# Sigmoid attention interleaved with a seven-product FFN: operands' parts and sums in other slots, PSUM banks kept across the first stage change, another opening

## The chip, the cores and the metric

The kernel runs on one core of one Trainium2 chip. The metric is the device time of one execution in microseconds, as the median of several runs. On a core, TensorE (PE) multiplies matrices, VectorE (DVE) and ScalarE (ACT) work elementwise, GpSimd (POOL) does next to nothing here, and SyncE (SP) issues nearly all DMA transfers. Each engine executes its own instructions in order and waits on semaphores for the others.

## The reference

Shapes: q, k, v are 8 x 12 x 448 x 64 (batch, heads, sequence, head size), w_in is 768 x 2048, w_out 2048 x 768.

```
scores = (1 / sqrt(64)) * q @ k.T - log(448)
attn   = 1 / (1 + exp(-scores))
x      = (attn @ v), heads joined: 3584 x 768
h      = x @ w_in
g      = max(0.01 * h, h)
out    = g @ w_out
```

The weights come in as 64-bit floats; the kernel decodes them on the chip.

## The kernel before, in words

**Precision.** Every operand of a product is split into a high part (a copy rounded to fp32r, ScalarE's `high`) and a low part (the rest, a subtraction, VectorE's `low`), and each product is made as three: high with high, high with low, low with high (`parts_mm`, line 157). For q and k the tile of both parts is `qks`, for the FFN's left operands `so`, for its weights `w`.

**Attention.** Two heads make a pair of 128 partitions; there are 48 pairs, 12 to a quarter. `load_qk` and `load_v` load a pair's operands; `split` (pair 0 alone) or `high` and `low` make the parts of q and k; `scores(h)` makes two tiles of scores (`sc`) and two sigmoids on ScalarE (`s`), `attn_v(h)` the products with v into a bank `pv`, and `keep` copies a finished bank to `x`.

**FFN.** Both products use a scheme over 2 x 2 blocks with seven block products instead of eight, taken in the order 0, 1, 4, 5, 3, 6, 2. The left operand of the first product consists of seven combinations of blocks of x (class `Operands`): operand n has a high part, a low part, and some need a sum first (`sum1`, `sum2`, `sum4`, `s3`). `Quad` gathers the results in the PSUM banks px and pz and adds them up into c11, c21, c22 and c12 (in the trace all named `c_h`): after product 5 ScalarE copies pz into c22, after product 3 VectorE adds px to it, which frees px for product 2. `First.after` then issues the activation, the sums s3, s4, s2 of the results (in the trace `s<-c_h`, `s<-s`) and their stores `g<-c_h`, `g<-s`. A block of nine matmuls is one of the seven products for one of eight column groups u.

**The order.** Attention of quarter q runs between the steps of the first product of quarter q - 1: 56 steps p0 to p55, with slots e0.0 to e12.3 for the pairs; in quarter 0 there is attention alone, and the second product comes after everything. `slot` runs the chores that `later` has put down for it, then its work. The tables `PLAN` (line 473) and `PLAN_ALONE` (line 477, quarter 0) say in which slot a step of `Operands` is issued: `"p50": "h102"` is the high part of operand 1, thirds 0 to 2, in step 50; l is a low part, s a sum, and a key that begins with n is a slot of the next quarter. All instructions are pinned to the order in which the program issues them.

**Weights.** The generator `prep` (line 247) decodes 16 blocks, w_in's and w_out's, on VectorE: each step is one instruction. The raw halves or quarters `wr` become `wd`, then four differences `ws` are made; three parts of `wd` and all of `ws` are stored to DRAM (`t`), from where `Weights` reads them (`wx`). After each block come some empty steps, `WAIT[0]` for the first four blocks, `WAIT[1]` for the others, as the next block takes memory that the stores must have read. The first four blocks' raw parts lie in the buffers of `so`. `prepare` advances the generator by `PACES` steps per slot: the first value in quarter 0, the second until w_in is done, the third behind it.

**Banks and loads.** PSUM has eight banks. In quarter 0 the pool `ps_a` has three tiles of two banks for scores and two for pv; at quarter 1 it is closed and `ps_b` opened, with two score tiles, two pv, px and pz (line 607). At the start (line 566) SyncE issues k of pair 0 in halves, q and k of pair 1, then v_0, v_1, q and k of pair 2 and v_2; ScalarE issues q of pair 0.

Every instruction in the trace has line 90, that of the helper that pins it, so rows are told apart by their tiles.

Of the kernel before, what the change touches and what calls it, by code (L numbers as in the profile page):

```python
# [9 lines left out]
F32 = mybir.dt.float32  # L10
# [6 lines left out]
P = 128  # L17
# [7 lines left out]
ST = 9  # L25
# [1 line left out]
ALONE = 4  # L27


PACES = 1.45, 2.2, 1.33  # L30
WAIT = 2, 4


JOINT_ALONE = 1, 3, 5, 7
# [22 lines left out]
def attn_ffn_kernel(ctx: ExitStack, tc: tile.TileContext, qk, v, w_in, w_out, out):  # L57
# [153 lines left out]

    ps = ExitStack()

    def banks(name, sizes):

        pool = ps.enter_context(tc.tile_pool(name=name, bufs=1, space=PSUM, reuse_waits="tile"))
# [101 lines left out]

    xs = {}

    KEYS = slice(0, S // 2), slice(S // 2, S)
    OTHERWISE = 9

    class Pair:
# [32 lines left out]
        def split(self):  # L357

            self.parts = spl.tile([P, 2, 2, S], F32R, tag="qks", name=f"qks_{self.i}")
            high, low = self.parts[:, 0], self.parts[:, 1]  # L360
            copy(out=high[:, 0], in_=self.raw[:, 0])
            vcopy(out=high[:, 1, KEYS[0]], in_=self.raw[:, 1, KEYS[0]])
            sub(low[:, 0], self.raw[:, 0], high[:, 0])
            for n, cols in enumerate(KEYS):
                if n > 0:
                    vcopy(out=high[:, 1, cols], in_=self.raw[:, 1, cols])
                sub(low[:, 1, cols], self.raw[:, 1, cols], high[:, 1, cols])

        def scores(self, h):
            todo, acts = [], []  # L370
            for c in range(2 * h, 2 * h + 2):
                ps = psum("s", f"sc_{self.i}_{c}")

                if self.part == 0:
                    k0, n, rows = c * KR, KR, slice(0, KR)
                elif c < NK - 1:
                    k0, n, rows = c * P, P, slice(0, P)
                elif self.part == 1:
                    k0, n, rows = S - D, D, slice(0, D)
                else:  # L380
                    k0, n, rows = S - P, P, slice(D, P)
                for m, (kp, qp) in enumerate(((0, 0), (0, 1), (1, 0))):
                    for j, me in enumerate(heads):
                        todo.append((c, m, dict(out=ps[:n, j, :S], lhsT=self.parts[me, kp, 1, k0:k0 + n],
                                                rhs=self.parts[me, qp, 0], start=m == 0, stop=m == 2)))
# [12 lines left out]

        def attn_v(self, h):
            if h == 0:  # L400
                self.pv = psum("pv", f"pv_{self.i}")
# [23 lines left out]
    class Operands:  # L425
# [45 lines left out]


    PLAN = {
# [3 lines left out]
    PLAN_ALONE = {  # L477
# [3 lines left out]


    w1 = []
# [26 lines left out]
    class First:  # L510
# [22 lines left out]
        def after(self, quad, c, u, n):  # L533
            got = quad.done(n)
            if got is None:
                return
            p = self.p
            row, col, t = got
            c[row, col] = t

            def save(n, t):
                dma(out=gd[p][n][:, u], in_=t)

            def sums(n, fn, x, y):
                c[n] = st.tile([P, S], F32, tag="st", name=f"s{n}_{p}_{u}", bufs=ST)
                fn(c[n], c[x], c[y])

            if n != 2:
                later(1, lambda: leaky(t, t))
            if n == 1:  # L550
                later(3, lambda: save(0, t))
            elif n == 3:
                later(3, lambda: save(6, t))
            elif n == 6:
                later(2, lambda: sums(3, add, (1, 0), (1, 1)))
                later(3, lambda: sums(4, sub, 3, (0, 0)))
                later(4, lambda: save(3, c[3]))
                later(4, lambda: sub(t, c[0, 0], t))
                later(5, lambda: save(4, c[4]))
                later(6, lambda: save(5, t))  # L560
            else:
                later(2, lambda: save(1, t))
                later(4, lambda: sums(2, sub, (0, 1), 4))
                later(6, lambda: save(2, c[2]))
# [38 lines left out]
    for q in range(NQ + 1):  # L603
        before, ops = ops, Operands(q) if q < NQ else None
        if q == 0:
            slot(lambda: pairs[0].scores(0))
        elif q == 1:
            ps.close()
            psum = banks("ps_b", dict(s=(2, 2), pv=(2, 1), px=(1, 1), pz=(1, 1)))
        if q == 0:  # L610
            for j in range(per):
                i, busy = j, j == 0 or j >= per - 2
# [24 lines left out]
        for k in range(size):  # L637
# [10 lines left out]
                    later(1, pairs[i + 1].load_v)  # L648
            go(q, f"p{k}", first.step, k >= 50 or k < 7)
    ps.close()  # L650


    KS = 2
# [149 lines left out]
```

## Time and profile before

| | |
|---|---|
| median of 3 runs | 1111.12 us (1110.78 to 1113.02) |
| the profiled execution | 1110.32 us, its span 1108.5 us |
| granted TensorE clock, mean | 0.998 |
| busy: TensorE, VectorE, ScalarE | 1093.0, 666.4, 614.3 us |
| DMA | 250.09 MB, mean 226 GB/s |

The profile is of one execution. A timeline row has start and length in us, the engine, the operation with the tile that it writes and those that it reads, its shape and count, and in brackets the idle time before it with what ended that. Rows of like instructions in a row are drawn together. A row of waits has the waiting engine and tile, what was waited for, the total in us, the count and the longest.

### The profile page before, as it was taken

How to read it: one execution, taken by the hardware profiler on the slowest of the kernel's cores; microseconds unless marked ns; L12 is line 12 of the kernel's file. 1: busy time of each engine (PE TensorE's matmuls, PEld its weight loads, DVE VectorE, ACT ScalarE, POOL GpSimd, SP SyncE). 2: the span in 40 equal slices, each digit the busy share in tenths (PEclk: the TensorE clock that was granted, in tenths of full speed). 3: DMA queues.
4: the chain of work that ended last, by engine and by line, in shares of the span. 5: the costliest groups of instructions: out<-in, count | busy, mean ns of one | idle time of the engine just before them, and what ended most of it. 6: DMA issues, size and time to landing. Idle time of an engine off the chain costs nothing.

```text
span 1108.5 us, 15979 instructions
## 1 busy us (share of the span) xinstructions
PE 1093.0 (99%) x5952; PEld 893.6 (81%) x5952; DVE 666.4 (60%) x987; ACT 614.3 (55%) x862; POOL 0.3 (0%) x5
## 2 busy tenths in 40 slices
PE   8999999999999999999999999999999999999998
PEld 4556767777777777777778899999999999999998
DVE  5889888768676678676568666655433333343332
ACT  7886666677666667665667555554333333323331
POOL 0000000000000000000000000000000000000000
PEclk9999999999999999999999999999999999999999
DMA  7966988885787786777755889786645554454552
GB/s 276 342 205 226 326 282 300 282 280 166 232 287 279 249 253 203 251 262 257 259 200 147 284 265 297 273 287 213 203 142 157 158 171 154 133 176 150 157 149 92
DMA packets 105133, 250.09 MB, mean 226 GB/s; under 512 B 11680, under 2 KB 54816, under 8 KB 105056
## 3 DMA queue, kind: packets, MB, share of 16 engines
q1 hardware_dynamic: 104912, 248.85, 68.2%
q8 instruction: 46, 0.75, 0.3%
q14 instruction: 31, 0.25, 0.1%
q10 hardware_dynamic: 144, 0.23, 0.1%
HBM read 164.63 MB, written 84.41 MB: 225 GB/s over the span
## 4 chain that ended last, share of the span: by engine, by line
PE 92%; DVE 3%; ACT 2%; DMA 1%; issue 1%; SPq 0%; DVEq 0%; ACTq 0%
PE px_o L90 21%; PE px_h L90 19%; PE pv L90 12%; PE sc L90 11%; PE pz_o L90 10%; PE pz_h L90 9%; PE py_o L90 5%; PE py_h L90 5%; ACT s L90 1%; DVE so L90 1%; ACT so L90 1%; DMA t<-wd 1%; DVE w L90 1%; DVE x L90 0%; DMA g<-s 0%
## 5 line engine op out<-in xcount | busy, mean ns | idle before, releaser
L90 DVE TENSOR_TENSOR gs<-gg,gs 128x896 fp32r<-128x896 f32 x112 | 122.2, 1092 | 226.9 <-ACT gs L90 226.7
L90 PE MATMUL px_h<-so,w 128*128 128x448 f32 x1152 | 250.9, 366 | 1.4 <-DVE c_h L90 1.1
L90 PEld LDWEIGHTS px_h<-so,w 128*128 128x128 f32 x1152 | 213.4, 188 | 27.9 <-issue 8.2
L90 PE MATMUL px_o<-gs,w 128*128 128x448 f32 x1152 | 232.5, 362 | 0.0
L90 ACT CAST gs<-gg 128x896 fp32r<-128x896 f32 x112 | 105.3, 941 | 222.5 <-PE px_o L90 117.6
L90 PEld LDWEIGHTS px_o<-gs,w 128*128 128x128 f32 x1152 | 216.0, 187 | 14.4
L90 ACT ACTIVATE s<-sc 128x896 f32<-128x896 f32 (+1 forms) x192 | 171.6, 918 | 72.3 <-PE sc L90 49.4
L90 PE MATMUL sc<-qks 64*128 64x448 f32 (+2 forms) x1152 | 144.0, 385 | 8.0 <-ACT qks L90 4.3
L90 PEld LDWEIGHTS sc<-qks 64*128 64x128 f32 (+2 forms) x1152 | 98.1, 180 | 65.1 <-issue 28.2
L90 DVE TENSOR_TENSOR w<-wx,w 128x768 fp32r<-128x768 f32 (+1 forms) x160 | 136.1, 853 | 16.3 <-ACT w L90 14.7
L90 PE MATMUL pv<-s,v 128*64 128x448 f32 (+2 forms) x768 | 141.9, 551 | 0.0
L90 PE MATMUL pz_h<-so,w 128*128 128x448 f32 x576 | 126.6, 363 | 2.6 <-DVE c_h L90 1.3
L90 ACT CAST w<-wx 128x768 fp32r<-128x768 f32 (+1 forms) x160 | 119.8, 752 | 5.7 <-DMA wx<-t 5.3
L90 PEld LDWEIGHTS pz_h<-so,w 128*128 128x128 f32 x576 | 107.4, 187 | 12.2 <-ACT c_h L90 1.9
L90 PE MATMUL pz_o<-gs,w 128*128 128x448 f32 x576 | 116.5, 362 | 0.0
L90 PEld LDWEIGHTS pz_o<-gs,w 128*128 128x128 f32 x576 | 108.0, 187 | 7.2
L90 PEld LDWEIGHTS pv<-s,v 128*64 128x64 f32 (+2 forms) x768 | 42.8, 135 | 76.7 <-issue 74.6
L90 DVE TENSOR_TENSOR qks<-qk,qks 128x896 fp32r<-128x896 f32 (+2 forms) x50 | 52.5, 1052 | 38.4 <-ACT qks L90 38.3
L90 DVE SCALAR_TENSOR_TENSOR wd<-wr,wd 128x384 int32<-128x384 int32 (+1 forms) x112 | 68.6, 613 | 2.3
L90 ACT COPY c_h<-px_h 128x448 f32<-128x448 f32 x64 | 34.1, 533 | 60.7 <-PE px_h L90 59.8
L90 ACT ACTIVATE c_h<-c_h 128x448 f32<-128x448 f32 x96 | 55.2, 575 | 22.1 <-DVE c_h L90 22.1
L90 PE MATMUL py_h<-so,w 128*128 128x448 f32 x288 | 62.9, 362 | 0.0
(38 smaller groups left out, 663.0 us busy)
## 6 DMA issues: line engine op xcount, KB each, us to landing
gg<-g SPq DMA_DIRECT2D x112, 448.0 KB, 3.5
wx<-t SPq DMA_DIRECT2D x120, 384.0 KB, 4.1
g<-c_h SPq DMA_DIRECT2D x128, 224.0 KB, 4.9
g<-s SPq DMA_DIRECT2D x96, 224.0 KB, 4.9
qk<-in_qk SPq DMA_DIRECT2D x47, 448.0 KB, 5.1
t<-ws SPq DMA_DIRECT2D x16, 768.0 KB, 5.4
wr<-in_w_out SPq DMA_DIRECT2D x32, 384.0 KB, 4.6
out<-c_o SPq DMA_DIRECT2D x48, 224.0 KB, 2.0
```

Source lines behind the costliest of these rows:

```text
L90: return lambda *args, **kw: tc.keep_in_program_order(issue(*args, **kw))
```

## The change

- **Parts and sums.** In `PLAN`, operand 2's high part moves from np3 to np4 and is made in two pieces, its low part from np4 to np4 and np5 in two pieces; a third of the sum for operand 4 that operand 2 rests on moves from np2 to e12.2; sums 1 and 2 are split likewise. In `PLAN_ALONE`, operand 2's high part moves from ne1.0 to ne1.3, its low part from ne1.2 to np4.
- **Results' sums.** For a quarter's last column group, s4, the subtraction into c21, s2 and their stores come four slots later (`LATER`).
- **Weights.** The paces in quarters 1 and later are 2.45 and 1.46 (2.2 and 1.33); seven empty steps follow a block from the fifth on (four).
- **Banks.** pv and two of the score tiles lie in pools of their own, kept from quarter 0 to the end of the first product's attention; only the third score tile's two banks are given to px and pz.
- **Opening.** q and k of pair 0 are loaded in halves, q's by ScalarE, k's by SyncE; pair 1's likewise, q by ScalarE; v_1 and v_2 come behind q and k of pairs 2 and 3. `split` works in halves of columns. Pair 0's first scores are made in halves of columns, the first tile finished ahead of the second. Before them stand seven products of zeros (64 x 112, into a pv bank that is not read).

```
-PACES = 1.45, 2.2, 1.33
-WAIT = 2, 4
+PACES = 1.45, 2.45, 1.46
+LATER = 4
+IDLE = 7
+WAIT = 2, 7
...
             if self.i == 0:
-                dma_act(out=self.raw[:, 0], in_=qk[self.i, :, 0])
-                for cols in KEYS:
-                    dma(out=self.raw[:, 1, cols], in_=qk[self.i, :, 1, cols])
+                for cols in HALVES:
+                    dma_act(out=self.raw[:, 0, cols], in_=qk[self.i, :, 0, cols])
+                    dma(out=self.raw[:, 1, cols], in_=qk[self.i, :, 1, cols])
+            elif self.i == 1:
+                dma_act(out=self.raw[:, 0], in_=qk[self.i, :, 0])
+                dma(out=self.raw[:, 1], in_=qk[self.i, :, 1])
...
-                ps = psum("s", f"sc_{self.i}_{c}")
+                ps = psum_s(self.i * NK + c, f"sc_{self.i}_{c}")
...
+                for cols in HALVES if self.i == h == 0 else (slice(0, S),):
+                    for m, (kp, qp) in enumerate(((0, 0), (0, 1), (1, 0))):
+                        for j, me in enumerate(heads):
+                            todo.append((c, (m > 0 and c + 1, m, cols.start), dict(
...
-        "np0": "h302", "np1": "l302", "np2": "h602 s402", "np3": "l602 h202", "np4": "l202"}
+        "np0": "h302", "np1": "l302", "np2": "h602 s412", "np3": "l602", "np4": "h200 h212 l200", "np5": "l212"}
...
+                z = LATER if u == NU - 1 else 0
-                later(3, lambda: sums(4, sub, 3, (0, 0)))
+                later(3 + z, lambda: sums(4, sub, 3, (0, 0)))
...
+    zeros = st.tile([P, S], F32, tag="st", name="zeros", bufs=ST)[:, :S // 4]
+    nc.vector.memset(zeros, 0.0)
     pairs[0].load_qk()
     pairs[1].load_qk()
     pairs[0].load_v()
-    pairs[1].load_v()
     act(out=warm, in_=warm, func=AF.Sigmoid)
     pairs[0].split()
     pairs[2].load_qk()
+    pairs[1].load_v()
...
-    psum = banks("ps_a", dict(s=(3, 2), pv=(2, 1)))
+    psv = ExitStack()
+    psum_v = banks("ps_v", dict(pv=(2, 1)), psv)
+    psum_two = banks("ps_s", dict(s0=(1, 2), s1=(1, 2)), psv)
+    psum = banks("ps_a", dict(s2=(1, 2)))
+
+    def psum_s(n, name):
+
+        if n < per * NK:
+            return (psum if n % 3 == 2 else psum_two)(f"s{n % 3}", name)
+        return psum_two(f"s{n % 2}", name)
...
         if q == 0:
+            unread = psum_v("pv", "unread")
+            for _ in range(IDLE):
+                mm(unread[heads[0], :S // 4], lhsT=zeros[:, :D], rhs=zeros, start=True, stop=True)
             slot(lambda: pairs[0].scores(0))
         elif q == 1:
             ps.close()
-            psum = banks("ps_b", dict(s=(2, 2), pv=(2, 1), px=(1, 1), pz=(1, 1)))
+            psum = banks("ps_b", dict(px=(1, 1), pz=(1, 1)))
```

ScalarE at the first steps of the first product (quarter 1): c22 is the result block copied from pz, so2_0 operand 2 of quarter 0, s_13_0 to s_13_2 the sigmoids of pair 13. Before:

```order
L90 CAST w0_0_3_1004<-wx0_0_3_801 128x384
L90 COPY c22_h0_0_1016<-pz_h0_0_1006 128x448
L90 CAST so2_0_1020<-x_1_484 128x1344
L90 ACTIVATE s_13_0_1030<-sc_13_0_1022 128x896
L90 ACTIVATE s_13_1_1038<-sc_13_1_1023 128x896
L90 ACTIVATE s_13_2_1069<-sc_13_2_1061 128x896
```

Now:

```order
L92 CAST w0_0_3_1036<-wx0_0_3_833 128x384
L92 COPY c22_h0_0_1048<-pz_h0_0_1038 128x448
L92 ACTIVATE s_13_0_1060<-sc_13_0_1052 128x896
L92 ACTIVATE s_13_1_1068<-sc_13_1_1053 128x896
L92 CAST so2_0_1093<-x_1_516 128x1344
L92 ACTIVATE s_13_2_1103<-sc_13_2_1095 128x896
```

The cast of operand 2 has moved behind two sigmoids.

VectorE at the same place, from the sum for operand 2 (x_1) to the addition into c22; wr0_3, wd0_3 and ws0_3 belong to the fourth weight block. Before:

```order
L90 TENSOR_TENSOR x_1_484<-x_1_484,s2_0_831 128x1344
L90 SCALAR_TENSOR_TENSOR wd0_3_782<-wr0_3_0_595,wd0_3_782 128x768
L90 TENSOR_SCALAR wd0_3_782<-wr0_3_1_664 128x768
L90 TENSOR_SCALAR wd0_3_782<-wd0_3_782 128x768 x2
L90 TENSOR_TENSOR so2_0_1020<-x_1_484,so2_0_1020 128x1344
L90 SCALAR_TENSOR_TENSOR wd0_3_782<-wr0_3_1_664,wd0_3_782 128x768 x2
L90 TENSOR_TENSOR ws0_3_1079<-wd0_3_782 128x384
L90 TENSOR_TENSOR ws0_3_1079<-wd0_3_782,ws0_3_1079 128x384
L90 TENSOR_TENSOR w0_0_3_1004<-wx0_0_3_801,w0_0_3_1004 128x384
L90 TENSOR_TENSOR c22_h0_0_1016<-c22_h0_0_1016,px_h0_0_952 128x448
```

Now:

```order
L92 TENSOR_TENSOR x_1_516<-x_1_516,s2_0_863 128x1344
L92 SCALAR_TENSOR_TENSOR wd0_3_814<-wr0_3_0_627,wd0_3_814 128x768
L92 TENSOR_SCALAR wd0_3_814<-wr0_3_1_696 128x768
L92 TENSOR_SCALAR wd0_3_814<-wd0_3_814 128x768 x2
L92 SCALAR_TENSOR_TENSOR wd0_3_814<-wr0_3_1_696,wd0_3_814 128x768 x2
L92 TENSOR_TENSOR ws0_3_1091<-wd0_3_814 128x384
L92 TENSOR_TENSOR ws0_3_1091<-wd0_3_814,ws0_3_1091 128x384
L92 TENSOR_TENSOR ws0_3_1091<-wd0_3_814 128x384
L92 TENSOR_TENSOR so2_0_1093<-x_1_516,so2_0_1093 128x1344
L92 TENSOR_TENSOR w0_0_3_1036<-wx0_0_3_833,w0_0_3_1036 128x384
L92 TENSOR_TENSOR c22_h0_0_1048<-c22_h0_0_1048,px_h0_0_984 128x448
```

Operand 2's low part has moved behind the weight block's steps, one more ws among them, and the addition stays behind them all.

VectorE at the end of the sixth weight block (wr0_5, wd0_5), whose store is issued behind the last row that writes wd0_5. Before:

```order
L90 TENSOR_TENSOR c21_h0_2_1444<-c21_h0_2_1444,pz_h0_2_1451 128x448
L90 TENSOR_TENSOR qks_18_1547<-qk_18_1312,qks_18_1547 128x896
L90 TENSOR_SCALAR wd0_5_1425<-wd0_5_1425 128x384
L90 SCALAR_TENSOR_TENSOR wd0_5_1425<-wr0_5_3_1462,wd0_5_1425 128x384
L90 TENSOR_TENSOR w0_3_1_1570<-wx0_3_1_1431,w0_3_1_1570 128x2x384
L90 SCALAR_TENSOR_TENSOR wd0_5_1425<-wr0_5_3_1462,wd0_5_1425 128x384
```

Now:

```order
L92 TENSOR_SCALAR wd0_5_1441<-wd0_5_1441 128x384 x2
L92 TENSOR_TENSOR c22_h0_2_1499<-c22_h0_2_1499,px_h0_2_1431 128x448
L92 TENSOR_TENSOR w0_3_0_1567<-wx0_3_0_1429,w0_3_0_1567 128x2x384
L92 SCALAR_TENSOR_TENSOR wd0_5_1441<-wr0_5_3_1477,wd0_5_1441 128x384 x2
L92 TENSOR_TENSOR c21_h0_2_1480<-c21_h0_2_1480,pz_h0_2_1487 128x448
L92 TENSOR_TENSOR qks_18_1584<-qk_18_1347,qks_18_1584 128x896
```

The block's last steps have moved ahead of the addition into c21, a q/k low part and a weight low part.

VectorE where the first product of quarter 3 starts, from the addition into c11 of its column group 0 to that into c22; s4_2_7, s2_2_7 and c21_h2_7 are results of the quarter before. Before:

```order
L90 TENSOR_TENSOR c11_h3_0_6073<-c11_h3_0_6073,py_h3_0_6081 128x448
L90 TENSOR_TENSOR s4_2_7_6092<-s3_2_7_6076,c11_h2_7_5933 128x448
L90 TENSOR_TENSOR x_13_4921<-x_13_4921,s2_3_5987 128x1344
L90 TENSOR_TENSOR w0_0_2_6079<-wx0_0_2_6012,w0_0_2_6079 128x2x384
L90 TENSOR_TENSOR c21_h2_7_5966<-c11_h2_7_5933,c21_h2_7_5966 128x448
L90 TENSOR_TENSOR so6_3_6095<-x_15_5766,so6_3_6095 128x1344
L90 TENSOR_TENSOR s2_2_7_6133<-c12_h2_7_6055,s4_2_7_6092 128x448
L90 TENSOR_TENSOR so2_3_6116<-x_13_4921,so2_3_6116 128x1344
L90 TENSOR_TENSOR w0_0_3_6118<-wx0_0_3_6026,w0_0_3_6118 128x384
L90 TENSOR_TENSOR c22_h3_0_6130<-c22_h3_0_6130,px_h3_0_6063 128x448
```

Now, on to the sum s4 of the quarter before:

```order
L92 TENSOR_TENSOR c11_h3_0_6117<-c11_h3_0_6117,py_h3_0_6125 128x448
L92 TENSOR_TENSOR x_13_4964<-x_13_4964,s2_3_5924 128x896
L92 TENSOR_TENSOR w0_0_2_6123<-wx0_0_2_6054,w0_0_2_6123 128x2x384
L92 TENSOR_TENSOR so6_3_6137<-x_15_5811,so6_3_6137 128x1344
L92 TENSOR_TENSOR so2_3_6171<-x_13_4964,so2_3_6171 128x448
L92 TENSOR_TENSOR w0_0_3_6157<-wx0_0_3_6068,w0_0_3_6157 128x384
L92 TENSOR_TENSOR c22_h3_0_6169<-c22_h3_0_6169,px_h3_0_6107 128x448
L92 TENSOR_TENSOR so2_3_6171<-x_13_4964,so2_3_6171 128x896
L92 TENSOR_TENSOR w0_1_0_6175<-wx0_1_0_6105,w0_1_0_6175 128x2x384
L92 TENSOR_TENSOR c21_h3_0_6152<-c21_h3_0_6152,pz_h3_0_6159 128x448
L92 TENSOR_TENSOR s4_2_7_6205<-s3_2_7_6120,c11_h2_7_5976 128x448
```

Ahead of the addition into c22 the three sums of the quarter before, a third of x_13's sum and two thirds of operand 2's low part are gone.

More of the change, by code (lines that the diff above doesn't have):

```diff
@@ L212, in attn_ffn_kernel, with banks @@
     ps = ExitStack()
-    def banks(name, sizes):
-        pool = ps.enter_context(tc.tile_pool(name=name, bufs=1, space=PSUM, reuse_waits="tile"))
+    def banks(name, sizes, stack=ps):
+        pool = stack.enter_context(tc.tile_pool(name=name, bufs=1, space=PSUM, reuse_waits="tile"))
         def psum(tag, name):
@@ L360, in split @@
             high, low = self.parts[:, 0], self.parts[:, 1]
[L361 to L366, printed above, removed]
+            for cols in HALVES:
+                copy(out=high[:, 0, cols], in_=self.raw[:, 0, cols])
+            for n, cols in enumerate(HALVES):
+                vcopy(out=high[:, 1, cols], in_=self.raw[:, 1, cols])
                 sub(low[:, 1, cols], self.raw[:, 1, cols], high[:, 1, cols])
+                if n == 0:
+                    for x in HALVES:
+                        sub(low[:, 0, x], self.raw[:, 0, x], high[:, 0, x])
         def scores(self, h):
@@ L381, in scores @@
                     k0, n, rows = S - P, P, slice(D, P)
[L382 to L385, printed above, removed]
+                for cols in HALVES if self.i == h == 0 else (slice(0, S),):
+                    for m, (kp, qp) in enumerate(((0, 0), (0, 1), (1, 0))):
+                        for j, me in enumerate(heads):
+                            todo.append((c, (m > 0 and c + 1, m, cols.start), dict(
+                                out=ps[:n, j, cols], lhsT=self.parts[me, kp, 1, k0:k0 + n],
+                                rhs=self.parts[me, qp, 0, cols], start=m == 0 and cols.start == 0,
+                                stop=m == 2 and cols.stop == S, skip_group_check=True)))
                 acts.append((c, rows, ps))
@@ L554, in after @@
             elif n == 6:
+                z = LATER if u == NU - 1 else 0
                 later(2, lambda: sums(3, add, (1, 0), (1, 1)))
-                later(3, lambda: sums(4, sub, 3, (0, 0)))
+                later(3 + z, lambda: sums(4, sub, 3, (0, 0)))
                 later(4, lambda: save(3, c[3]))
-                later(4, lambda: sub(t, c[0, 0], t))
-                later(5, lambda: save(4, c[4]))
-                later(6, lambda: save(5, t))
+                later(4 + z, lambda: sub(t, c[0, 0], t))
+                later(5 + z, lambda: save(4, c[4]))
+                later(6 + z, lambda: save(5, t))
             else:
+                z = LATER if u == NU - 1 else 0
                 later(2, lambda: save(1, t))
-                later(4, lambda: sums(2, sub, (0, 1), 4))
-                later(6, lambda: save(2, c[2]))
+                later(4 + z, lambda: sums(2, sub, (0, 1), 4))
+                later(6 + z, lambda: save(2, c[2]))
     per = 2 * NP
@@ L650, in attn_ffn_kernel @@
     ps.close()
+    psv.close()
     KS = 2
```

4 lines of the change are left out of this document (2 added, 2 removed), and 6 rows, old and new, of tables (PLAN, PLAN_ALONE).

## The prediction

> **What bounds the kernel now.** I read the page first, then what TensorE waited for, then the timeline around each wait. The page gives span and TensorE's share; in its group row the last figures are busy us and mean ns of one:
>
> ```profile
> span 1108.5 us, 15979 instructions
> PE 1093.0 (99%) x5952; PEld 893.6 (81%) x5952; DVE 666.4 (60%) x987; ACT 614.3 (55%) x862; POOL 0.3 (0%) x5
> L90 PE MATMUL px_h<-so,w 128*128 128x448 f32 x1152 | 250.9, 366 | 1.4 <-DVE c_h L90 1.1
> ```
>
> TensorE's products fill the span, and the change leaves their number alone but for a few of zeros. It can only win what TensorE loses waiting. All its waits (engine, tile, what ended it: us, times, longest), then a row of the chain that ended last (start, length):
>
> ```profile
> PE sc L90 <- ACT qks L90: 4.3, 1, 4.3
> PE sc L90 <- ACT s L90: 3.6, 3, 2.7
> PE pz_h L90 <- DVE c_h L90: 1.3, 1, 1.3
> PE pz_h L90 <- ACT c_h L90: 1.2, 2, 0.6
> PE px_h L90 <- DVE c_h L90: 1.1, 1, 1.1
> PE px_h L90 <- DVE w L90: 0.3, 1, 0.3
> ```
> ```profile
> 158.84 1.80 PE px_h L90 x9
> ```
>
> Nine products take 1.80, 0.20 each, while the mean row says 0.366: each end is drawn 0.17 late. So a wait shown as X costs X + 0.17, and I work with starts: what should follow nine products starts 1.80 after them.
>
> **The start.** The timeline (start, length, engine, operation; in brackets the idle time before and its end):
>
> ```profile
> 2.11 1.38 SPq L90 DMA_DIRECT2D v<-in_v  x3
> 4.34 5.81 PE L90 MATMUL sc<-qks 64*112 64x448 f32 x36 [4.34 <-ACT qks L90]
> 6.59 3.34 ACT L90 ACTIVATE s<-sc 112x896 f32<-112x896 f32 x4 [2.31 <-PE sc L90]
> 7.05 0.63 DVE L90 CAST qks<-qk 128x896 fp32r<-128x896 f32 x1 [1.18 <-DMA qk<-in_qk]
> 7.71 1.09 DVE L90 TENSOR_TENSOR qks<-qk,qks 128x896 fp32r<-128x896 f32 x1
> 10.08 3.23 PE L90 MATMUL pv<-s,v 112*64 112x448 f32 x16
> ```
> ```profile
> 6.00:7.00 1.00, 1.00 (x8) 0.86 (x6) 0.00 (x0) 0.41 (x1) 0.00 (x0) 1.00 1.11 282
> ```
>
> The second pair's q and k land at 7.05 (VectorE waits for the DMA), and pair 0's attn_v starts 3.03 behind that. The window row (last three: granted clock, DMA share, GB/s) shows the DMA engines full at 282 GB/s just before, with v_0, v_1 and v_2 in flight. The change moves v_1 and v_2 behind the q/k loads: 448 KB by the kernel's shapes, 1.6 us of those engines if all of it went ahead, nothing if none did. I take 1.1: landing at 5.9, attn_v at 8.9.
>
> The other chain is ScalarE's. The first sigmoid starts at 6.59, 2.25 behind the first product, when 10 of pair 0's 12 first products are done. Now 8 of 12 (16 of 24 halves) complete the first tile, 2.25 x 8 / 10 = 1.8, and the first product starts some 0.3 earlier, since ScalarE casts half as much ahead of it: sigmoids from about 5.8, 0.8 earlier; at the pace without the wait for the low parts, 5.5. The last scores ahead of attn_v take the bank that the third sigmoid leaves, at 6.59 + 0.75 x 3.34 = 9.1, and attn_v starts 1.0 behind it; from 5.5 on that gives 9.0. So both chains end near 9.0: 1.1 gained, bounds 0 and 1.5.
>
> The seven products of zeros are not in the trace. The nearest row has 16 in 3.07 us, 0.2 for 448 columns, two instructions to a product: by columns 0.1 for one of 112, by the whole row 0.4, 0.7 to 2.8 together; from about 1.0 on they end before 4.34 either way, so nothing. At half clock and without regard to columns they would take 5.6 and cost 2.3.
>
> The Trainium skill, page "DMA: Bandwidth & Descriptors", section "Issuing engines are not separate DMA queues", speaks against half of this edit: transfers issued from ScalarE and SyncE run on the same 16 engines, and a second issuer saves only issue time. By it, were the second queue the whole edit, the start's 1.1 would be 0; the window agrees with its premise, since the engines are full, and my 1.1 rests on the order of the loads.
>
> **The bank change** (first product's start). ScalarE, TensorE and VectorE there, and one window:
>
> ```profile
> 73.43 0.87 PE L90 MATMUL sc<-qks 64*128 64x448 f32 x6 [0.64 <-ACT s L90]
> 86.21 1.49 PE L90 MATMUL sc<-qks 64*128 64x448 f32 x12
> 87.63 2.48 PE L90 MATMUL pv<-s,v 128*64 128x448 f32 x12
> 90.59 1.31 ACT L90 CAST so<-x 128x1344 fp32r<-128x1344 f32 x1 [2.89 <-DVE wd L90]
> 92.77 2.61 PE L90 MATMUL sc<-qks 64*128 64x448 f32 x12 [2.67 <-ACT s L90]
> 95.31 2.35 PE L90 MATMUL px_h<-so,w 128*128 128x448 f32 x9
> 95.58 0.56 DVE L90 TENSOR_TENSOR ws<-wd 128x384 f32<-128x384 f32 x1
> 97.50 1.96 PE L90 MATMUL pz_h<-so,w 128*128 128x448 f32 x9
> 97.70 0.62 DVE L90 TENSOR_TENSOR c_h<-c_h,px_h 128x448 f32<-128x448 f32 x1 [0.50 <-PE px_h L90]
> ```
> ```profile
> 94.00:95.00 1.00, 1.00 (x8) 0.69 (x6) 0.96 (x2) 0.70 (x1) 0.00 (x0) 0.50 0.68 264
> ```
>
> Two waits go. The scores at 73.43 waited for the last sigmoid of quarter 0, because all pools of banks were closed and opened anew; with the banks kept they wait for the one before, 0.64 + 0.17 = 0.8 earlier. The cast of operand 2 on ScalarE waited 2.89 for VectorE to read a weight block whose memory it takes, with two sigmoids behind it, and TensorE stood for 2.67. Then the clock was half for some 3 us: 12 scores took 95.31 - 92.77 = 2.54 where 87.63 - 86.21 = 1.42 is usual, and nine products 2.19 instead of 1.80. In all 2.67 + 0.17 + 1.12 + 0.39 = 4.35.
>
> Not all of it comes back. VectorE is busy there without a break until 97.70 - 0.50 = 97.20, and the addition into c22 at 97.70, which frees the bank for the next products (97.50 + 1.80 = 99.30), stands behind all that, and after the change behind one more sum of weights (0.56). VectorE reaches it at 97.20 + 0.56 - 0.80 = 96.96, ends at 97.58, and the products start at 97.65: 1.65 earlier instead of 0.8 + 4.35 = 5.15. TensorE, rid of its waits, has done attn_v (2.31), the scores and two blocks of nine at 87.63 - 0.80 + 2.31 + 1.42 + 1.80 + 1.80 = 94.16: a new wait of 3.5 in place of the 2.67. If this too halves the clock, it costs what it cost before, 1.12 + 0.39 = 1.5, and 0.15 is left; I take 0.2, bounds 0 and 1.65.
>
> The Trainium skill, page "TensorE: Matmul & The Clock Gate", section "Part 1: The HAM clock gate", says the clock is halved after at least one idle window of about 3.4 us. The page calls that window free-running, so a wait of 3.5 would hardly ever hold a whole one: by it the clock would stay full and the sum would be 1.5 better. The trace differs, with 0.50 after 2.67 of idle, and I follow the row.
>
> **The weight blocks' wait.** VectorE, TensorE and SyncE's issue:
>
> ```profile
> 145.59 0.95 DVE L90 TENSOR_TENSOR w<-wx,w 128x768 fp32r<-128x768 f32 x1
> 148.36 0.44 SPq L90 DMA_DIRECT2D t<-wd  x1
> 153.50 1.96 PE L90 MATMUL px_h<-so,w 128*128 128x448 f32 x9
> 155.03 0.36 DVE L90 TENSOR_SCALAR wd<-wr 128x384 int32<-128x384 int32 x1 [2.41 <-DMA t<-wd]
> 156.76 2.08 PE L90 MATMUL pz_h<-so,w 128*128 128x448 f32 x9 [1.30 <-DVE c_h L90]
> ```
>
> The next block's first step waited 2.41 for the store of the one before, and the addition that TensorE needs stood behind it: 156.76 - 153.50 - 1.80 = 1.46. Now the store's last input stands ahead of an addition, a q/k low part and a weight low part (0.62 + 1.09 + 0.95): 2.66 earlier, over 2.41. Gain 1.46. Bounds: all, or none if the faster pace eats the distance.
>
> **The quarters' boundaries.**
>
> ```profile
> 268.92 1.96 PE L90 MATMUL px_h<-so,w 128*128 128x448 f32 x9
> 269.26 1.32 ACT L90 CAST so<-x 128x1344 fp32r<-128x1344 f32 x1
> 271.47 2.07 PE L90 MATMUL pz_h<-so,w 128*128 128x448 f32 x9 [0.59 <-ACT c_h L90]
> ```
>
> 271.47 - 268.92 - 1.80 = 0.75, because the copy of c22 stood behind operand 2's cast (1.32), twice by the waits' row. The cast now stands behind the copy: two times 0.75, 1.5; 0.75 if only one place clears.
>
> **The last quarter.**
>
> ```profile
> 606.52 1.68 PE L90 MATMUL px_h<-so,w 128*128 128x448 f32 x7 [0.29 <-DVE w L90]
> 608.03 2.37 PE L90 MATMUL pz_h<-so,w 128*128 128x448 f32 x9
> 608.92 1.55 DVE L90 TENSOR_TENSOR so<-x,so 128x1344 fp32r<-128x1344 f32 x1
> 611.53 1.68 PE L90 MATMUL px_h<-so,w 128*128 128x448 f32 x7 [1.12 <-DVE c_h L90]
> ```
>
> Lost: 0.29 + 0.17 = 0.46; 608.03 - 606.52 - 1.40 = 0.11; 611.53 - 608.03 - 1.80 = 1.70; 2.27. VectorE has too much at once. Now a third of operand 4's sum (of the size of the 1.55) comes earlier, two sums of results and a subtraction (of the size of the 0.62) four slots later, and two thirds of operand 2's low part behind the c22 addition: 0.5 + 1.9 + 1.0 = 3.4 leave the stretch ahead of that addition, more than the 2.27 lost. I keep 0.2 for a new wait behind the two thirds: 2.1. Bounds 0 to 2.3: the delayed sum takes a buffer that a store must have left, and what is queued behind it on VectorE would wait with it.
>
> **Sum.** 1.1 + 0.2 + 1.46 + 1.5 + 2.1 = 6.4. The profiled execution took 1110.32 (its span and 1.8 around it); less 6.4 is 1103.9. The median of the runs, 1111.12, is 0.8 above it: 1104.7.
>
> **Rivals.** (1) The clock stays full after the new wait of 3.5: 6.4 + 1.5 = 7.9, 1103.2. For it: the wait lies elsewhere than the 2.67, and where a wait falls may matter; against: it is the longer one. By the clock page's rule above this is what happens. Chance 0.17. (2) Only part comes: the second pair lands late, the bank change gives nothing, the last quarter's wait moves on: 1.46 + 1.5 = 3.0, 1108.2. For it, the full DMA engines and VectorE's unbroken work. 0.18. (3) The bank change gives all of 5.15, VectorE not being late: 6.4 + 4.95 = 11.3, 1099.8; 0.05. (4) The change doesn't do what it says, each wait being replaced by an equal one: 1111.1; 0.06. (5) Slower: VectorE blocks at a weight block's first step more often than now. The pace of steps rises by a tenth, so stores and reuse of their memory come closer; eleven later blocks take that path, each wait costs 1.46. From five on (7.3 over 6.4) the kernel is slower; six give 8.8 - 6.4 = 2.4, 1113.5. Against it, it happened once, with four empty steps where seven now stand. 0.06.
>
> **How the numbers follow.** The forecast holds 0.48: 1104.7. The range starts below rival 1 with the start's and the last quarter's best (1103.2 - 0.4 - 0.2) and the 0.8 between run and median: 1101.8. It ends just behind rival 2: 1108.4. That leaves out rivals 3 to 5, 0.17, and the rim of 2. A measurement here can tell 0.2% (2.2 us) from no change. Faster by more: 0.48 + 0.17 + 0.05 and most of rival 2, 0.85; within it rival 4 and the rest of 2, 0.09; slower 0.06.
>
> **What would show it.** Right: attn_v of pair 0 near 9.0; no wait at 73; a wait of about 3.5 for the c22 addition where 92.77 was, with the clock at half or not deciding between forecast and rival 1; nothing near 155, 270 and 443; at most 0.3 near 610. Wrong: a VectorE wait for a weight store anywhere new, q and k of pair 1 still at 7, or ScalarE behind VectorE at 90.

## The result, and the profile after

The changed kernel took 1105.84 us (median of 4 runs, 1103.42 to 1106.88), the kernel before 1110.98 beside it (4 runs, 1110.78 to 1113.02): a ratio of 0.9946, interval 0.9926 to 0.9967. The forecast was 1104.7. The profiled execution took 1105.26, its span 1103.5, 5.04 less than before. First what TensorE waits for now (engine, tile, what ended the wait: us, times, longest):

```profile
PE px_h L92 <- DVE c_h L92: 3.1, 1, 3.1
PE unread L92 <- DVE zeros L586: 1.0, 1, 1.0
PE sc L92 <- DVE qks L92: 0.6, 1, 0.6
PE sc L92 <- ACT s L92: 0.3, 1, 0.3
PE pv L92 <- DMA v<-in_v: 0.2, 1, 0.2
PE sc L92 <- ACT qks L92: 0.2, 1, 0.2
```

Most of before's waits are gone. A new one of 3.1 for the addition into c22 is the only long one; the others are small, at the opening and for a v. VectorE's row where the second pair's q and k land (start, length, operation, idle before), then the timeline of TensorE at the places that the prediction named (start, length, operation, count, idle before):

```profile
7.19 0.63 DVE L92 CAST qks<-qk 128x896 fp32r<-128x896 f32 x1 [1.60 <-DMA qk<-in_qk]
```
```profile
10.22 3.23 PE L92 MATMUL pv<-s,v 112*64 112x448 f32 x16
73.82 2.48 PE L92 MATMUL pv<-s,v 112*64 112x448 f32 x12 [0.17 <-DMA v<-in_v]
92.96 1.96 PE L92 MATMUL pz_h<-so,w 128*128 128x448 f32 x9
98.06 5.44 PE L92 MATMUL px_h<-so,w 128*128 128x448 f32 x18 [3.14 <-DVE c_h L92]
153.99 1.96 PE L92 MATMUL px_h<-so,w 128*128 128x448 f32 x9
155.79 1.96 PE L92 MATMUL pz_h<-so,w 128*128 128x448 f32 x9
269.62 1.96 PE L92 MATMUL pz_h<-so,w 128*128 128x448 f32 x9
441.35 1.96 PE L92 MATMUL pz_h<-so,w 128*128 128x448 f32 x9
606.51 3.76 PE L92 MATMUL px_h<-so,w 128*128 128x448 f32 x18
```

Set beside the starts of the same instructions before, these rows give the whole account. Attn_v of pair 0 starts at 10.22, 0.14 later than before. The products behind c22 start at 98.06, 1.24 earlier than 99.30. Then the clock is halved, and the rows at 153.99 (before 153.50) are 0.49 later. From there on it is all gain: 155.79 is 0.97 earlier than 156.76, 269.62 is 1.85 earlier than 271.47, 441.35 is 2.63 earlier than 443.98 (the second of before's waits for c22's copy), 606.51 is 5.02 earlier than 611.53, and so it stays to the end. The row of before that the prediction does not show:

```profile
443.98 2.08 PE L90 MATMUL pz_h<-so,w 128*128 128x448 f32 x9 [0.59 <-ACT c_h L90]
```

VectorE and the clock at the new wait:

```profile
95.36 1.55 DVE L92 TENSOR_TENSOR so<-x,so 128x1344 fp32r<-128x1344 f32 x1
96.83 0.56 DVE L92 TENSOR_TENSOR w<-wx,w 128x384 fp32r<-128x384 f32 x1
97.30 0.62 DVE L92 TENSOR_TENSOR c_h<-c_h,px_h 128x448 f32<-128x448 f32 x1
```
```profile
98.00:99.00 1.00, 0.94 (x3) 0.89 (x4) 1.00 (x2) 1.00 (x2) 0.00 (x0) 0.53 0.52 101
99.00:100.00 1.00, 1.00 (x4) 0.91 (x3) 1.00 (x2) 0.25 (x1) 0.00 (x0) 0.50 0.95 346
100.00:101.00 1.00, 1.00 (x4) 0.87 (x4) 1.00 (x2) 0.00 (x0) 0.00 (x0) 0.50 0.81 240
101.00:102.00 1.00, 1.00 (x6) 0.91 (x5) 0.66 (x2) 0.28 (x1) 0.00 (x0) 0.77 0.27 100
```

VectorE has no idle time ahead of the addition; as forecast, it comes late behind the weight block's steps. The third column from the right is the granted clock: half for 3.4 us behind the wait. In the four runs the mean clock and span were 1.000 and 1101.6, 0.998 and 1103.5, 0.997 and 1104.5, 0.997 and 1105.1: by its mean clock, one of them was not halved there at all.

### The profile page after: what moved, and what is told of

Same layout as the page of the kernel before. It is cut to its first block, busy times and chain, and to the rows that moved or that the text cites. A ratio compares the mean times of both kernels' runs of the same rounds, so it can differ in the third digit from the quotient of the medians.

```text
span 1103.5 us, 16033 instructions
## 1 busy us (share of the span) xinstructions
PE 1094.4 (99%) x5978; PEld 898.2 (81%) x5978; DVE 669.2 (61%) x998; ACT 614.5 (56%) x866; POOL 0.3 (0%) x5
## 4 chain that ended last, share of the span: by engine, by line
PE 94%; DVE 3%; ACT 1%; DMA 1%; issue 1%; ACTq 0%; SPq 0%; DVEq 0%
PE px_h L92 21%; PE px_o L92 21%; PE pv L92 11%; PE pz_o L92 10%; PE pz_h L92 10%; PE sc L92 10%; PE py_h L92 5%; PE py_o L92 5%; DVE wd L92 1%; DVE so L92 1%; DVE qks L92 1%; DMA qk<-in_qk 0%; ACT s L92 0%; DMA v<-in_v 0%; ACT so L92 0%
## 5 line engine op out<-in xcount | busy, mean ns | idle before, releaser
L92 PE MATMUL sc<-qks 64*128 64x448 f32 (+3 forms) x1164 | 142.6, 380 | 1.1 <-DVE qks L92 0.6
L92 DVE TENSOR_TENSOR qks<-qk,qks 128x896 fp32r<-128x896 f32 (+1 forms) x51 | 52.7, 1034 | 33.1 <-ACT qks L92 32.8
```

The source lines that it names most:

```text
L92: return lambda *args, **kw: tc.keep_in_program_order(issue(*args, **kw))
```

## The experiments

Each is an edit of the changed kernel. Where times differ by less than the runs spread, the starts in the traces decide.

**The opening.** e1_opening_old puts the opening of before in its place:

```
+                dma_act(out=self.raw[:, 0], in_=qk[self.i, :, 0])
                 for cols in HALVES:
-                    dma_act(out=self.raw[:, 0, cols], in_=qk[self.i, :, 0, cols])
                     dma(out=self.raw[:, 1, cols], in_=qk[self.i, :, 1, cols])
-            elif self.i == 1:
-                dma_act(out=self.raw[:, 0], in_=qk[self.i, :, 0])
-                dma(out=self.raw[:, 1], in_=qk[self.i, :, 1])
...
     pairs[0].load_v()
+    pairs[1].load_v()
...
```

> The changed kernel with the opening of before (loads, split and first scores as before, no products of zeros); all else as changed. Theory A, from the two traces: the new opening wins nothing, since the second pair's q and k landed at 7.19 after and 7.05 before; so attn_v of pair 0 starts at 10.1 (10.22 in the changed kernel) and the time is the changed kernel's within 0.3 us. Rival, the prediction's term: the opening is worth 1.1, which the landing of that one execution hid; then this kernel is 1.1 us slower than the changed one.

1105.57 us (1105.15 to 1106.08), against 1105.84; span 1103.3. VectorE and TensorE of its timeline:

```profile
6.69 0.63 DVE L92 CAST qks<-qk 128x896 fp32r<-128x896 f32 x1 [0.71 <-DMA qk<-in_qk]
```
```profile
10.46 3.23 PE L92 MATMUL pv<-s,v 112*64 112x448 f32 x16
```

The second pair landed at 6.69 here, ahead of the changed kernel's 7.19. But the first scores ran slower, the first sigmoid started at 6.70 instead of 6.09, and attn_v of pair 0 came 0.24 later than in the changed kernel. At 73.82 both were level again, as the changed kernel waits there for a v. The same opening gave 10.08 in before's trace, so two executions of it lie 0.38 apart, more than the 0.24. The opening is worth nothing at the end, and at its own place no gain is shown, where 1.1 was forecast.

e2_v0_late issues v_0 later:

```
-    pairs[0].load_v()
     act(out=warm, in_=warm, func=AF.Sigmoid)
     pairs[0].split()
     pairs[2].load_qk()
+    pairs[0].load_v()
     pairs[1].load_v()
```

> The changed kernel with v_0 issued behind q and k of pair 2, as v_1 is. Theory A: packets of v_0 begin 1.6 us before the second pair's last ones end and share the DMA engines with them; without v_0 the second pair lands 0.5 to 0.8 earlier, near 6.5, and attn_v of pair 0 starts 0.5 earlier, unless v_0 itself lands after 9.7 and becomes the wait. Rival: the landing is set by something else (the packets' own pace on the slowest DMA engine), stays at 7.1, and attn_v of pair 0 stays at 10.2 or later.

1104.25 us (1103.78 to 1105.42). VectorE and TensorE of its timeline:

```profile
6.50 0.63 DVE L92 CAST qks<-qk 128x896 fp32r<-128x896 f32 x1 [1.07 <-DMA qk<-in_qk]
```
```profile
9.52 3.23 PE L92 MATMUL pv<-s,v 112*64 112x448 f32 x16
19.11 2.49 PE L92 MATMUL sc<-qks 64*128 64x448 f32 x18 [0.42 <-ACT s L92]
```

The theory held: 6.50 instead of 7.19, and attn_v 0.70 earlier. That is clear of the spread: in the ten profiled executions that have the changed kernel's loads up to v_0 in their order, the second pair lands between 7.10 and 7.64, and e10_v0_behind_too, which moves v_0 as well, has 6.50 again. So v_0 is the load that costs the second pair time here; with v_1 and v_2 out of the way, but v_0 not, the landing is no earlier than before's 7.05. At 19.11 a wait for a sigmoid takes the 0.70 back; at the end the span is 1103.6, 0.15 above the changed kernel's.

e12_no_zeros leaves the products of zeros out:

```
-            for _ in range(IDLE):
+            for _ in range(0):
```

> The changed kernel without the seven products of zeros. Theory: they only raise the clock for the first scores (spaced 0.2 a pair of heads from 5.5 on where before they were 0.37 apart until 7.1); the first sigmoid then comes some 0.5 later without them, but the second pair's landing at 7.2 sets attn_v of pair 0, so the time is the same within 0.3 us. Rival: the sigmoids' chain sets it, and 0.5 to 1 is lost.

1106.78 us (1106.06 to 1107.76). VectorE:

```profile
7.49 0.63 DVE L92 CAST qks<-qk 128x896 fp32r<-128x896 f32 x1 [2.02 <-DMA qk<-in_qk]
```

Attn_v of pair 0 starts at 10.52 instead of 10.22, 3.03 behind the landing in both traces. The 0.30 is the landing's, which varies as much with the zeros in place, so nothing is shown to be the zeros' worth. The landing sets the start, as the theory had it; its other part did not come, as the first sigmoid starts at 6.00, no later than the 6.09 with zeros. The other 0.7 of the 1.0 between the spans is a wait of 0.82 for v at 74.78, the same that the next experiment shows with zeros; it is not theirs.

**The bank change.** e3_pause takes weight steps out of the way. The added line takes effect behind slot e1.0, so for e1.1 to e1.3 alone, and by the traces seven steps leave the stretch ahead of the addition, not the eight expected:

```
                 i, busy = q * per + j, j in (0, per)
                 go(q, f"e{j}.0", (lambda: pairs[i].scores(0)) if i <= last else None, busy)
+                busy = busy or (q, j) == (1, 1)
```

> The changed kernel with the weights' generator not advanced in slots e1.0 to e1.3 of quarter 1, so that VectorE has eight steps of the fourth weight block less ahead of operand 2's low part and the addition into c22. Theory B: these steps are the whole cause of TensorE's wait of 3.14 at 98.06; the addition then ends ahead of TensorE, neither the wait nor the half clock behind it come, and the span falls by 3.3 + 1.6 = 4.9 against an execution that has both, to about 1098.5. Rival: the wait moves, either to operand 2's cast on ScalarE or to where the delayed weight steps fall; then 1.6 us or less is won.

1100.39 us (1100.10 to 1100.88), ratio to before 0.9900, 0.9885 to 0.9915. TensorE and VectorE of its timeline:

```profile
74.55 1.72 PE L92 MATMUL pv<-s,v 112*64 112x448 f32 x8 [0.81 <-DMA v<-in_v]
93.69 1.96 PE L92 MATMUL pz_h<-so,w 128*128 128x448 f32 x9
95.49 3.76 PE L92 MATMUL px_h<-so,w 128*128 128x448 f32 x18
```
```profile
92.26 1.56 DVE L92 TENSOR_TENSOR so<-x,so 128x1344 fp32r<-128x1344 f32 x1 [0.92 <-ACT so L92]
94.21 0.62 DVE L92 TENSOR_TENSOR c_h<-c_h,px_h 128x448 f32<-128x448 f32 x1
```

The addition now runs at 94.21, TensorE goes from 93.69 to 95.49 without a gap, and the clock was 1.000 in all four runs, which lie within 0.8 us. So these seven steps, 4.7 us of VectorE's time (90.65 to 95.36 in the changed kernel), were what made it late; with them behind the addition no other wait takes the place. The span is 1099.1 and not 1098.5 since the wait for v, 0.17 in the changed kernel, was 0.81 in this execution.

e4_cast_early puts operand 2's parts of quarter 0 back:

```
-        "np0": "h422 l422 s102", "np1": "h302", "np2": "l302 h602", "np3": "l602 s402", "ne1.3": "h202", "np4": "l202"}
+        "np0": "h422 l422 s102", "np1": "h302", "np2": "l302 h602", "np3": "l602 s402", "ne1.0": "h202", "ne1.2": "l202"}
```

> The changed kernel with operand 2's parts of quarter 0 in the slots of before (high part in ne1.0, low part in ne1.2). Theory B: moving them only handed the wait from one place to the other; here ScalarE stands for VectorE again ahead of two sigmoids, TensorE waits about 2.7 at 92 instead of 3.1 at 98, the clock is halved once either way, and the span is the changed kernel's within 0.5 us. Rival: the move did win something; then this kernel is 1 to 3 us slower.

1104.19 us (1103.46 to 1104.92). ScalarE and TensorE:

```profile
89.93 1.31 ACT L92 CAST so<-x 128x1344 fp32r<-128x1344 f32 x1 [2.90 <-DVE wd L92]
```
```profile
92.12 1.68 PE L92 MATMUL sc<-qks 64*128 64x448 f32 x12 [2.67 <-ACT s L92]
99.02 3.16 PE L92 MATMUL px_h<-so,w 128*128 128x448 f32 x15
```

The old wait of 2.67 is back and the new one is gone; the span is 1102.9, 0.56 below the changed kernel's, 0.25 of it won ahead of 74. This part of the change only handed the wait on, as the forecast had it, and won nothing.

e8_pause_v11 is e3_pause with v_11 loaded one slot earlier:

```
-                    if j == (x - 2 if x < per - 1 else x - 1):
+                    if x != per - 1 and j == (x - 2 if x < per - 1 else x - 1):
...
+                if j == per - 3:
+                    pairs[per - 1].load_v()
                 if per - 6 <= j < per - 2:
```

> As e3_pause, and v_11 is loaded one slot earlier, ahead of a weight load and of q and k of pair 13 in SyncE's queue. In e3_pause TensorE waits at 74.55 for v_11, 0.81 by the trace and 0.97 by the starts; in the changed kernel 0.17 and 0.34. Theory: this landing has taken the place of the sigmoid's wait that the kept banks removed, so it goes: span 0.6 to 1.0 below that of e3_pause with its 1099.1, and below 1098.0 in the best run. Rival: q and k of pair 13, now later, or the sigmoids become the wait there, and no more than 0.2 is won.

The profiled span is 1098.2, 0.85 below e3_pause, all of it at 74:

```profile
73.69 3.23 PE L92 MATMUL pv<-s,v 112*64 112x448 f32 x16
```

Nothing took the place of that wait: where the kept banks end the wait for a sigmoid, the landing of v_11 had become the next one. The median does not show it, 1100.68 us (1099.75 to 1101.43): two of the four spans were 1098.2 and 1098.0, two 1099.5 and 1099.6.

e11_banks_old is e8_pause_v11 with before's pools:

```
-    psum_v = banks("ps_v", dict(pv=(2, 1)), psv)
-    psum_two = banks("ps_s", dict(s0=(1, 2), s1=(1, 2)), psv)
-    psum = banks("ps_a", dict(s2=(1, 2)))
+    psum = banks("ps_a", dict(s=(3, 2), pv=(2, 1)))
...
-            psum = banks("ps_b", dict(px=(1, 1), pz=(1, 1)))
+            psum = banks("ps_b", dict(s=(2, 2), pv=(2, 1), px=(1, 1), pz=(1, 1)))
```

> As e8_pause_v11, with the pools of banks of before (all closed and opened anew at quarter 1). Theory: the scores at 73 wait for the last sigmoid of quarter 0 again, 0.8 by the trace of before, and nothing behind it makes up for it: 0.8 slower than e8_pause_v11 at that place, span near 1099.0. Rival: the kept banks are worth nothing, as another wait follows at once: within 0.2.

1100.05 us (1099.84 to 1100.42), span 1098.1. TensorE:

```profile
70.74 2.69 PE L92 MATMUL sc<-qks 64*112 64x448 f32 x24
73.50 3.23 PE L92 MATMUL pv<-s,v 112*64 112x448 f32 x16
```

There is no wait for a sigmoid within the 24 products of scores, so the theory fell: in this program closing all pools costs nothing. A reading that fits is that in this program, where the products of zeros ask for a pv bank first, the pools lay their tiles out in another order than before, and the second new score tile lies on a bank that was free by then; what cost 0.8 before was then which old tile lay there. It is thus no exact undoing, and neither the layout nor its cause was tried by itself.

**The other terms.** e5_sums_on_time:

```
-LATER = 4
+LATER = 0
```

> The changed kernel with LATER = 0: the three sums of the quarter before (0.62 each) stand ahead of the addition into c22 again at 598 to 606. In the changed kernel that addition ends at 605.76, 0.75 ahead of TensorE at 606.51, and VectorE has 0.42 idle ahead of it. Theory: 1.86 more on VectorE, less 0.42, less 0.75, leaves TensorE a wait of 0.7 and the time 0.7 longer; the split of operand 2's low part and of operand 4's sum did the rest of the 2.39 won there. Rival: the delay of the sums did it all; then TensorE loses 2.3 again.

1105.36 us (1104.22 to 1106.70). This execution was 0.20 behind the changed kernel since its opening, and here its block starts 0.68 behind 606.51:

```profile
607.19 3.99 PE L92 MATMUL px_h<-so,w 128*128 128x448 f32 x18 [0.28 <-DVE c_h L92]
```

The wait is 0.28 + 0.17 = 0.45, and with what the products behind it lose the span is 0.7 longer than those 0.20, as the theory had it (1104.4). The delay of the sums is under a third of what was won there. The rest is put down to operand 2's low part and operand 4's sum by subtraction; no run gives back both, and e7_plan_old below gives back the first alone and loses nothing.

e6_four_empty:

```
-WAIT = 2, 7
+WAIT = 2, 4
```

> The changed kernel with WAIT = 2, 4 (the new paces stay). This is the slower rival of the prediction at work: every later block's first step comes three steps, 2.2 us, nearer to the store of the block before. At the sixth block the store lands about 0.4 ahead of that step in the changed kernel, so VectorE waits 1.8 there, and at some of the other ten blocks. Theory: TensorE loses 0.5 to 1.5 at each place where an addition stands behind, 1.5 to 4 in all. Rival: the new pace alone moved the steps, the empty steps do nothing; then no change over 0.3.

1106.27 us (1104.15 to 1109.14). VectorE waited for a store four times, 6.3 us in all. One of these, 0.17 at 30.77, is among the first blocks, whose empty steps are the same; the others are 2.54, 1.69 and 1.94 at 129.73, 173.91 and 196.30. Only the first of the three cost TensorE anything, 1.00 at 134.66 (134.66 - 131.86 - 1.80). The last VectorE row here is the first step behind the sixth block, where before waited 2.41:

```profile
DVE wd L92 <- DMA t<-wd: 6.3, 4, 2.5
129.73 0.36 DVE L92 TENSOR_SCALAR wd<-wr 128x384 int32<-128x384 int32 x1 [2.54 <-DMA t<-wd]
151.35 0.35 DVE L92 TENSOR_SCALAR wd<-wr 128x384 int32<-128x384 int32 x1
```
```profile
131.86 1.97 PE L92 MATMUL px_h<-so,w 128*128 128x448 f32 x9
134.66 2.08 PE L92 MATMUL pz_h<-so,w 128*128 128x448 f32 x9 [0.83 <-DVE c_h L92]
```

Another 0.37 goes at 148.71, where no such wait is near: three `ws` steps now stand ahead of an addition that stood ahead of them. That is 1.4 in all, just under the theory's 1.5 to 4. And the wait behind the sixth block does not come back: with four empty steps and the new pace its store lands at 150.45, ahead of the step at 151.35. So at the place that the prediction named the three more empty steps are not needed, the new pace being enough there; they keep the wait away from three others. In the changed kernel this store is issued at 144.53 (before 148.36) and lands at 149.69, 1.95 ahead of the step:

```profile
144.53 0.42 SPq L92 DMA_DIRECT2D t<-wd  x1
```
```profile
151.64 0.35 DVE L92 TENSOR_SCALAR wd<-wr 128x384 int32<-128x384 int32 x1
```

The rest of this execution's 3.9 lies elsewhere: 1.2 more lost at half clock, which lasted 6.8 us here, and 1.3 in the first 21 us, most of it where ScalarE's cast of pair 3 waits for its load:

```profile
18.40 0.94 ACT L92 CAST qks<-qk 128x896 fp32r<-128x896 f32 x1 [2.01 <-DMA qk<-in_qk]
```

e7_plan_old:

```
-        "np0": "h302", "np1": "l302", "np2": "h602 s412", "np3": "l602", "np4": "h200 h212 l200", "np5": "l212"}
+        "np0": "h302", "np1": "l302", "np2": "h602 s412", "np3": "l602 h202", "np4": "l202"}
```

> The changed kernel with operand 2's parts of quarters 1 to 3 in np3 and np4 in one piece, as before (the sums stay as changed). Theory: the copy of c22 stands behind the cast of 1.32 again in quarters 2 and 3 and TensorE loses 0.75 to 0.85 at 269 and at 441, 1.6 together; in the last quarter 1.03 of low part comes back ahead of the addition into c22, of which 0.42 and 0.75 are covered, so nothing more. Rival: the last quarter's 2.39 goes too, or half of it; then 2.8 to 4 are lost.

1107.19 us (1105.12 to 1107.60). Both waits are back, and the last quarter loses nothing:

```profile
270.24 2.08 PE L92 MATMUL pz_h<-so,w 128*128 128x448 f32 x9 [0.59 <-ACT c_h L92]
442.83 2.08 PE L92 MATMUL pz_h<-so,w 128*128 128x448 f32 x9 [0.59 <-ACT c_h L92]
```

The span is 1.6 longer, as expected.

**Taking the rest.** e9_weights_behind is e8_pause_v11 with the first two weight loads behind q and k of pair 3:

```
-    next(preps)
     pairs[1].high(vcopy)
     pairs[1].low()
     pairs[3].load_qk()
+    next(preps)
```

> As e8_pause_v11, and the first two weight loads (1536 KB together) are issued behind q and k of pair 3 instead of ahead. Theory: in some executions ScalarE's cast of pair 3 waits for its q and k, queued behind these loads (TensorE lost 1.27 at 20 in the run with four empty steps, 0.4 in the one with v_0 behind); this is what spreads e8's spans from 1098.0 to 1099.6. Then all spans lie within 0.5 of 1098.0. Rival: the spread comes from elsewhere and stays, or VectorE's first decoding step, now later, holds up the low parts behind it and 0.5 or more is lost.

1100.20 us (1099.81 to 1102.14), spans 1098.9, 1098.0, 1100.4, 1098.4, 1098.4. The theory did not hold: the spread stayed. In the profiled execution there is a wait at a place that no other showed, 612.64 - 610.30 - 1.80 = 0.54, for a copy of c22 on ScalarE that waited for a store to leave its buffer:

```profile
612.05 0.53 ACT L92 COPY c_h<-pz_h 128x448 f32<-128x448 f32 x1 [1.95 <-DMA g<-c_h]
```
```profile
610.30 1.97 PE L92 MATMUL px_h<-so,w 128*128 128x448 f32 x9
612.64 2.08 PE L92 MATMUL pz_h<-so,w 128*128 128x448 f32 x9 [0.37 <-ACT c_h L92]
```

The prediction named a wait of this kind, for a buffer that a store must have left, as a bound of its last term. The span of 1100.4 goes with a clock of 0.998. What spreads the spans is not settled.

e10_v0_behind_too adds e2_v0_late's edit to it.

> As e9_weights_behind, and v_0 is issued behind q and k of pair 2. Theory: what e2_v0_late won at the start (0.7: pair 1 landed at 6.5) was lost again at 19 behind the weight loads, which now come later; so 0.5 to 0.7 stays, spans near 1097.4. Rival: v_0 or a sigmoid is the next wait and nothing stays.

1099.61 us (1099.36 to 1099.65), ratio to before 0.9896, 0.9882 to 0.9910, the best of all. TensorE:

```profile
9.67 3.23 PE L92 MATMUL pv<-s,v 112*64 112x448 f32 x16
15.58 2.48 PE L92 MATMUL pv<-s,v 128*64 128x448 f32 x12
17.99 2.83 PE L92 MATMUL sc<-qks 64*128 64x448 f32 x24
```

Attn_v starts 0.68 earlier than in e8_pause_v11, passes 18 without a wait, and the 0.7 stays to the end: span 1097.6, all four within 0.3. The opening could win its 0.7, with v_0 and the first weight loads out of the way of q and k.

## Why the prediction was right, and where it was off

The forecast was 1104.7 for 1105.84, and 6.4 of gain for 5.04 in the traces. By the starts quoted above, three terms were right in mechanism and near in size, one in mechanism only, and one failed. The first two came out below the lower bound of 0 that each was given. The number was near all the same, as together they were 1.3 of the 6.4, and the others brought 0.45 more than forecast. In part it was chance: whether the half clock comes decides 1.7 us of an execution.

- **The start: 1.1 forecast, -0.14 came.** This step failed: "The change moves v_1 and v_2 behind the q/k loads ... I take 1.1: landing at 5.9". The 0.14 is less than the 0.38 by which two executions of the old opening differ, so no loss is shown either. The landing was 7.19, which the prediction had named as a sign of being wrong ("q and k of pair 1 still at 7"). Engines that are full while v_0, v_1 and v_2 are in flight do not say which of the three is worth moving; e2_v0_late shows that it is v_0, which the change left in place. Why the landing did not come earlier with v_1 and v_2 gone stays open: the change also divides the second pair's load between two issuing engines, and no run undoes that by itself. The other chain brought part of its gain (sigmoids from 6.09, where 6.59 was and 5.8 forecast), but attn_v needs both. By the Trainium skill, page "DMA: Bandwidth & Descriptors", section "Issuing engines are not separate DMA queues", a second issuing engine saves only the time of issuing. The trace agrees: half of the second pair's load was issued by ScalarE, and it landed at 7.19, no earlier than the 7.05 before.
- **The bank change: 0.2 forecast, -0.49 + 0.14 = -0.35 came.** VectorE's lateness, the place and the half clock came as forecast; the wait was 3.31 (3.14 + 0.17) where 3.5 was forecast. The step that was off is "0.64 + 0.17 = 0.8 earlier": the landing of v_11 and the later start took half of it, 0.41 being left at 73.82, so VectorE reached the addition at 97.30 instead of 96.96. Its cause, that all pools were closed, was not enough by itself, as e11_banks_old shows. The half clock cost 1.24 + 0.49 = 1.73 behind 98.06, a little more than the 1.5 taken. By their mean clock, rival 1 came true in one run of four, at 1103.42 where its price was 1103.2. By the rule of the Trainium skill, page "TensorE: Matmul & The Clock Gate", section "Part 1: The HAM clock gate", it would have been the usual case; three runs of four, at 0.997 and 0.998, differ.
- **The weight blocks' wait: 1.46 forecast, 0.97 + 0.49 = 1.46 came.** The step was right: the store is issued 3.83 earlier and lands ahead of the next block's first step. e6_four_empty shows that the new pace does this without the three more empty steps, and what the slower rival looks like: three waits of VectorE, one of which cost TensorE 1.00. The other two are covered.
- **The boundaries: 1.5 forecast, 1.85 - 0.97 = 0.88 and 2.63 - 1.85 = 0.78 came;** e7_plan_old gives them back.
- **The last quarter: 2.1 forecast, 5.02 - 2.63 = 2.39 came.** The new wait that was kept back, 0.2, did not come: VectorE was done ahead of TensorE (no wait at 606.51). e5_sums_on_time gives 0.7 of it to the delayed sums; how the rest is divided stays open.

## What to carry to other kernels

When one engine waits for a second that is itself late, moving the waiting step only hands the wait on; look for what can leave the late engine's queue (here seven weight steps that nothing needed then), and the wait goes, with the half clock behind it. Before a load is credited with an earlier landing, find by a run which other transfer holds it up: moving the wrong ones wins nothing. And where a wait is removed, ask the trace of before what stands close behind: v_11 landed there at 73.17, only 0.2 ahead of the end of the sigmoid that was waited for, and in the changed kernel and its variants that kept the load's place it landed between 0.07 ahead of that sigmoid's end and 0.91 behind it.

## What was not expected of the hardware

In the profiled executions the half clock comes with waits of TensorE of 2.67 to 3.15 and lasts 3.4 us, in e6_four_empty 6.8. By the mean clock it does not come in every execution: the changed kernel ran with a mean clock of 1.000 in one of four runs, e5_sums_on_time and e4_cast_early in two of four, e3_pause, without such a wait, in all four. The changed kernel's executions so lie up to 3.5 us apart (not all of it the clock's), those of e3_pause 0.8.

The traces show something more about when it comes. Within each trace the switches of the granted clock lie whole multiples of 3.413 us apart: in the changed kernel it rises at 5.90, falls at 98.06, which is 27 x 3.413 later, and rises again at 101.47. The fall keeps no fixed distance from the wait: it came at 92.50 in before's trace, 0.27 ahead of the end of the wait, and at 93.87 in e4_cast_early, 1.75 behind the end, with only 1.66 of the wait in the 3.41 us just before it. So less than 3.41 us of idle time is enough. If the clock is set only at such instants, by what TensorE did since the last one, the same wait can halve it in one execution and not in another, as it falls differently between them. No profiled execution has such a wait at full clock, so this is a reading and not shown.

And a wait costs a little behind itself too: nine products take 2.08 after one, as they do behind scores without one (91.04 in the changed kernel), and 1.96 behind other products of the FFN (442.83 in e7_plan_old, 441.35 in the changed kernel). So each wait between such products that goes wins 0.12 more, which the differences above count with the next term.
